# A fused attention and feed-forward kernel: the last product's lower half in two column halves, one tail store in one transfer, five stores in two

## The chip, the cores and the metric

The kernel runs on one core of a Trainium2 chip. A core has a matrix engine (TensorE, "PE" in the profile; its weight loads are listed apart as "PEld"), a vector engine (VectorE, "DVE"), a scalar engine (ScalarE, "ACT"), GpSimd ("POOL") and SyncE ("SP"), which does nothing here but issue transfers and wait. Transfers go through 16 DMA engines that the issuing queues share. The metric is the device time of one execution in microseconds (us). Before the change it is 294.83 us, the median of three runs (294.2 to 295.05).

## The reference

Eight batches of eight heads, 576 positions, head size 64. Attention looks back over a window of 64 positions; its output, 4608 rows of 512, goes through a feed-forward block with a squared ReLU.

```python
def attention(q, k, v):                 # (8, 8, 576, 64) each
    scores = np.matmul(q, k.transpose(0, 1, 3, 2)) / np.sqrt(64)
    rel = pos[:, None] - pos[None, :]
    scores = np.where((rel >= 0) & (rel < 64), scores, -1e9)
    attn = np.exp(scores - scores.max(-1, keepdims=True))
    return np.matmul(attn / attn.sum(-1, keepdims=True), v)

x = attention(q, k, v).transpose(0, 2, 1, 3).reshape(4608, 512)
h = np.maximum(x @ w_in, 0.0)           # w_in: 512 x 2048
out = (h * h) @ w_out                   # w_out: 2048 x 512
```

## The kernel before

The 4608 rows are worked in nine groups of 512. Groups 0 to 7 are the first 512 positions of each batch; group 8 holds the last 64 positions of all eight batches, two batches to a block of 128 rows. For each group the attention comes first (36 tiles of 128 rows in all), then the up-product into PSUM (`U`, line 482, in group 0, `UPm`, line 515, after it), ReLU on ScalarE and a square on ScalarE or VectorE, and then the down-product (`out_seven`, line 664).

The down-product treats 512 x 2048 times 2048 x 512 as two-by-two blocks and forms the result from seven block products instead of eight. The seven are listed in `plan` (line 738): a PSUM bank, the stationary operand, the moving one, and what is evicted after it. Sums of blocks of h are made on VectorE (`hsum`), sums of blocks of w_out once at the start. Each block product (`product`, line 685) is 16 matmuls: eight steps of K by two blocks `m` of 128 rows, 256 columns wide. `evac` (line 716) adds a bank to earlier sums and writes the result to one of three output buffers, `osb_all`; a buffer holds 256 rows of 512 columns, as two blocks of 128 rows.

`store` (line 703) sends a buffer to the output. In groups 0 to 7 it is one transfer of 512 KB from SP for each of the group's two halves (`row`), 16 transfers in all (line 706). In group 8, whose 128-row blocks hold 64 rows of each of two batches, every store is two transfers, 64 partitions each: one from SP, one from ScalarE's queue (line 712).

The last product of all is product 6 of group 8. Only there `by_rows` is set: all eight steps for the upper 128 rows come first, then all eight for the lower 128, and the two halves sit in different PSUM tiles (`split`). Each half is evicted on its own, 128 x 256, and stored on its own.

The order in which instructions are recorded is written out by hand in the string `ORDER` (line 15); each word is one step, and each engine works its own instructions in that order. `hs` is a sum, `Z` a half of a block product, `ev` an eviction, `sd` and `sh` a store. The last words are

```
Z8.5.1 sh8.1.1 Z8.6.0 ev8.5 Z8.6.1 sh8.0.1 ev8.6.0 sh8.1.0.0 ev8.6.1 sh8.1.0.1
```

So the last four are: evict and store the upper 128 rows of the last block, evict and store the lower 128. The waits are set by the layer that records the kernel: an instruction waits for a count of another engine's, and a transfer from SP or ScalarE's queue raises one of eight semaphores, taken in turn in the order of recording. A transfer also waits until the transfer eight before it, on the same semaphore, has landed. At the end SP waits for all eight in their order, drains, and all engines meet in a barrier (line 840).

Of the kernel before, what the change touches and what calls it, by code (L numbers as in the profile page):

```python
# [12 lines left out]
ALU = mybir.AluOpType  # L13
# [84 lines left out]
def kernel(  # L98
# [12 lines left out]
    nc = tc.nc  # L111
    B, H, S, D = q.shape
    NT, DM = out.shape
    DFF = moe_w_in.shape[1]
    P = 128
    HP = H // 2
    W_SCALE = 128.0
    OUT_SCALE = 1.0 / (W_SCALE * W_SCALE)
# [3 lines left out]
    NTB = NT // 512  # L122
# [3 lines left out]
    KH = FFC // 2  # L126
    NH = DM // 2
# [206 lines left out]
    def psum_of(kind):  # L334

        if kind in held:
            return held.pop(kind)
        if kind == "att":
            return ps_att.tile([P, 2, 512], FP32, name="att", tag="ps_a")
        if kind == "any":  # L340
            turns.append(len(turns) % 2)
            return psum_of(("up", "out")[turns[-1]])
        pool, tag = (ps_up, "ps_u") if kind == "up" else (ps_out, "ps_o")
        taken[kind] += 1
        return pool.tile([P, 512], FP32, name=tag, tag=tag)
# [295 lines left out]
    def next_osb():  # L641
        osbs.append(len(osbs) % 3)
        return osb_all[:, osbs[-1]]
# [20 lines left out]
    def out_seven(g):  # L664
        h2 = h2s[g]
        TH = 256
        top = (slice(0, TH), slice(0, KH)), (slice(0, TH), slice(KH, FFC))
        bot = (slice(TH, 512), slice(0, KH)), (slice(TH, 512), slice(KH, FFC))
        A = [[h2[:, ks, ts] for ts, ks in row] for row in (top, bot)]
        Sh = [hs_all[:, i] for i in range(2)]  # L670
        Sh += [A[1][0], A[0][1]]
        banks, sums, osb = {}, {}, {}

        def hsum(i, half, e=1):
            ks = slice(half * KH // 2, (half + 1) * KH // 2)
            x, y, op = ((A[1][0], A[1][1], ALU.add), (Sh[0], A[0][0], ALU.subtract),
                        (A[0][0], A[1][0], ALU.subtract), (A[0][1], Sh[1], ALU.subtract))[i]
            (nc.gpsimd, nc.vector)[e].tensor_tensor(  # L678
                out=Sh[i][:, ks], in0=x[:, ks], in1=y[:, ks], op=op)

        def split(bank):

            return g == NTB - 1 and bank == "D"

        def product(bank, a, w, half, first, by_rows):
            if first and half == 0:
                t = psum_of("up" if bank == "E" else "out")[:].rearrange("p (m d) -> p m d", m=2)
                banks[bank] = [t[:, m] for m in range(2)]
                if split(bank):
                    banks[bank][1] = psum_of("up")[:, 0:NH]  # L690
                else:
                    banks[bank].append(t)
            steps = [(kk, m) for kk in range(half * KH // 2, (half + 1) * KH // 2)
                     for m in range(2)]
            if by_rows:
                steps = [(kk, half) for kk in range(KH)]
            for kk, m in steps:
                nc.tensor.matmul(  # L698
                    banks[bank][m], a[:, kk, m * P:(m + 1) * P], w[:, kk],
                    start=(first and kk == 0 and (m == 0 or split(bank))), stop=(kk == KH - 1),  # L700
                    skip_group_check=True)

        def store(row, cols, ms):
            if g < NTB - 1:
                r0 = g * S + row * TH
                nc.sync.dma_start(
                    out=out[r0:r0 + TH, cols].rearrange("(m p) d -> p m d", p=P),
                    in_=osb[row][:, :, cols])
            else:
                tails = out.rearrange("(m j r) d -> j r m d", j=2, r=S)  # L710
                for j in range(2):
                    (nc.sync, nc.scalar)[j].dma_start(
                        out=tails[j, S - 64:S, 2 * row + ms.start:2 * row + ms.stop, cols],
                        in_=osb[row][64 * j:64 * j + 64, ms, cols])

        def evac(bank, to, add=None, row=0, col=0, ms=slice(0, 2)):
            if to == "osb":
                if row not in osb:
                    osb[row] = next_osb()
                dst = osb[row][:, ms, col * NH:(col + 1) * NH]  # L720
            else:
                sums[to] = stage.tile([P, 2, NH], FP32, name=to, tag="st")
                dst = sums[to][:]
            if ms == slice(0, 2):
                src, other = banks[bank][2], sums[add][:] if add else None
            else:
                src, other = banks[bank][ms.start], sums[add][:, ms.start]
                dst = dst[:, 0]
            if add is None:
                nc.scalar.activation(out=dst, in_=src, func=AF.Copy, scale=OUT_SCALE)  # L730
            else:
                nc.vector.scalar_tensor_tensor(  # L732
                    out=dst, in0=src, scalar=OUT_SCALE, in1=other, op0=ALU.mult, op1=ALU.add)

        W = [[w_out_sb[:, 0:KH, 0:NH], w_out_sb[:, 0:KH, NH:DM]],
             [w_out_sb[:, KH:FFC, 0:NH], w_out_sb[:, KH:FFC, NH:DM]]]
        last = g == NTB - 1
        plan = [
            ("A", A[0][0], W[0][0], True, (("A", "p1"),)),
            (("E", A[0][1], W[1][0], True, (("E", "osb", "p1", 0, 0),)) if last else  # L740
             ("A", A[0][1], W[1][0], False, (("A", "osb", None, 0, 0),))),
            ("B", Sh[1], wb[0], True, (("B", "u2", "p1"),)),
            ("C", Sh[0], W[0][1], True, (("C", "u4", "u2"),)),
            ("D", Sh[2], wb[1], True, (("D", "osb", "u4", 1, 1),)),
            ("C", Sh[3], W[1][1], False, (("C", "osb", "u2", 0, 1),)),
            ("D", A[1][1], wb[2], False, (("D", "osb", "u2", 1, 0),)),
        ]

        def mult(n, half):
            bank, a, w, first, _ = plan[n]  # L750

            product(bank, a, w, half, first, last and n == 6)

        def evacs(n, m=None):
            for e in plan[n][4]:
                if m is None and not split(e[0]):
                    evac(*e)
                for i in range(2) if m is None and split(e[0]) else () if m is None else (m,):
                    evac(*e, ms=slice(i, i + 1))

        def send(row, col=None, m=None):
            store(row, slice(0, DM) if col is None else slice(col * NH, (col + 1) * NH),
                  slice(0, 2) if m is None else slice(m, m + 1))

        return hsum, mult, evacs, send
# [3 lines left out]
    def seven(g):  # L769
        if g not in sevens:  # L770
            sevens[g] = out_seven(g)
        return sevens[g]
# [72 lines left out]
```

## Time and profile before

| | us |
|---|---|
| median of three runs | 294.83 |
| profiled execution, its own time | 295.02 |
| its span, first to last instruction | 293.3 |
| TensorE busy | 283.8 (97%) |
| VectorE busy | 202.4 (69%) |
| ScalarE busy | 190.7 (65%) |
| GpSimd busy | 107.2 (37%) |
| granted clock of TensorE | 1.0 |

The span runs from the first instruction to the last; the execution's own time has 1.7 us more around it. A row of a timeline is: start, duration (both us), engine ("q" behind it for a queue that issues), line of the kernel, operation, output and inputs, shape, count. A row of a DMA answer is: transfer, queue, count, size, and the us from its issue to its landing. A row of the stretches ("285.00:290.00 ...") has the busy time of each engine, then TensorE's granted clock, the mean busy share of the 16 DMA engines and the GB/s that they moved. A row of groups has the busy time of a group and, behind the comma, the mean ns of one.

### The profile page before, as it was taken

The numbers are of one execution on the slowest core, as the hardware profiler recorded it, in microseconds if no ns is written. First come the engines' busy times: TensorE is split into PE (matmuls) and PEld (weight loads), VectorE is DVE, ScalarE is ACT, GpSimd is POOL, SyncE is SP. The second block draws the span as 40 slices with busy tenths as digits, with TensorE's granted clock in tenths as the row PEclk, the third lists the DMA queues.
The fourth block names the chain that finished last, engine by engine and source line by source line (L and its number), as shares of the span: only waits on it lengthen the run. The fifth ranks groups of instructions, "written<-read, shape, count | busy, mean of one in ns | idle before, by whom it ended". The sixth has DMA issues, their size and how long they took to land.

```text
span 293.3 us, 7351 instructions
## 1 busy us (share of the span) xinstructions
PE 283.8 (97%) x2957; PEld 189.6 (65%) x2957; DVE 202.4 (69%) x362; ACT 190.7 (65%) x310; POOL 107.2 (37%) x164
## 2 busy tenths in 40 slices
PE   8879999999999999999999999999999999999994
PEld 3546676657876477556666676575765667865683
DVE  2696877989866789678836884886565746833572
ACT  3867888794345963687776928557856977156710
POOL 2559111674363436356446344463224400000000
PEclk9999999999999999999999999999999999999999
DMA  7999999887899999999997999799999931301114
GB/s 215 301 258 274 195 196 213 187 185 173 215 210 222 229 234 213 228 212 251 213 205 162 251 248 187 180 233 251 201 207 296 219 35 74 107 2 72 72 34 111
DMA packets 163617, 55.52 MB, mean 189 GB/s; under 512 B 149248, under 2 KB 159488, under 8 KB 163584
## 3 DMA queue, kind: packets, MB, share of 16 engines
q1 hardware_dynamic: 156400, 49.82, 77.2%
q0 software_dynamic: 5280, 4.19, 9.0%
q10 hardware_dynamic: 1904, 1.05, 1.2%
q8 instruction: 23, 0.38, 0.5%
q14 instruction: 10, 0.08, 0.1%
HBM read 38.80 MB, written 9.44 MB: 164 GB/s over the span
## 4 chain that ended last, share of the span: by engine, by line
PE 60%; DVE 0%; issue 0%
PE ps_u L518 29%; PE ps_o L698 26%; PE att L443 2%; PE att L418 2%; PE ps_u L698 1%; DVE osb_all L732 0%
## 5 line engine op out<-in xcount | busy, mean ns | idle before, releaser
L518 PE MATMUL ps_u<-xT,w_in_sb 128*128 128x512 f16 x512 | 122.2, 379 | 0.3
L497 ACT ACTIVATE hrelu<-ps_u 128x512 f32<-128x512 f32 x136 | 80.1, 593 | 53.3 <-PE ps_u L518 50.4
L698 PEld LDWEIGHTS <-h 128*128 128x128 f16 x720 | 69.5, 98 | 16.6
L518 PEld LDWEIGHTS <-w_in_sb 128*128 128x128 f16 x512 | 48.6, 98 | 48.0 <-issue 2.1
L512 DVE SCALAR_TENSOR_TENSOR h<-ps_u,hrelu 128x512 f16<-128x512 f32 x55 | 37.6, 687 | 29.1 <-ACT hrelu L497 28.8
L508 ACT ACTIVATE h<-hrelu 128x512 f16<-128x512 f32 x85 | 53.0, 629 | 2.2
L698 PE MATMUL ps_o<-w_out_sb,h 128*128 128x256 f16 x416 | 52.2, 273 | 0.0
L425 ACT ACTIVATE pm<-att 128x1024 f16<-128x1024 f32 x36 | 35.9, 1021 | 8.5 <-PE att L418 8.4
L264 POOL CAST v_ev<-v_st 128x512 f16<-128x512 f32 x34 | 22.7, 668 | 43.4 <-DMA v_st<-in_v_dram 27.2
L698 PE MATMUL ps_o<-wb_all,h 128*128 128x256 f16 x272 | 35.3, 273 | 0.0
L264 POOL CAST k<-k_st 128x512 f16<-128x512 f32 x32 | 22.6, 707 | 32.3 <-DMA k_st<-in_k_dram 28.5
L698 PEld LDWEIGHTS <-hs_all 128*128 128x128 f16 x288 | 28.1, 98 | 6.6 <-issue 0.3
L264 POOL CAST q<-q_st 128x512 f16<-128x512 f32 x28 | 19.8, 707 | 31.2 <-DMA q_st<-in_q_dram 30.1
L430 DVE TENSOR_TENSOR pm<-pm,mask_inner 128x1024 f16<-128x1024 f16 x28 | 23.1, 827 | 10.3 <-ACT pm L425 10.0
L264 POOL COPY v_od<-v_ev 64x512 f16<-64x512 f16 x40 | 28.5, 714 | 2.5
L450 DVE TENSOR_TENSOR x_sb<-att,rden 128x512 f16<-128x512 f32 x36 | 24.9, 691 | 1.2
L732 DVE SCALAR_TENSOR_TENSOR osb_all<-ps_o,u 128x512 f32<-128x512 f32 (+1 forms) x27 | 18.0, 667 | 10.3 <-PE ps_o L698 10.1
L678 DVE TENSOR_TENSOR hs_all<-h 128x1024 f16<-128x1024 f16 x18 | 13.4, 747 | 8.0 <-ACT h L508 8.0
L698 PE MATMUL ps_o<-wb_all,hs_all 128*128 128x256 f16 x144 | 18.3, 273 | 0.0
L698 PE MATMUL ps_o<-w_out_sb,hs_all 128*128 128x256 f16 x144 | 17.7, 272 | 0.1
L678 DVE TENSOR_TENSOR h<-h,hs_all 128x1024 f16<-128x1024 f16 x18 | 13.8, 779 | 2.7 <-PE ps_o L698 2.4
L443 PEld LDWEIGHTS <-pm 128*64 128x64 f16 x576 | 11.0, 110 | 7.0 <-issue 4.3
(86 smaller groups left out, 251.8 us busy)
## 6 DMA issues: line engine op xcount, KB each, us to landing
k_st<-in_k_dram SPq DMA_DIRECT2D x39, 256.0 KB, 4.2
v_st<-in_v_dram SPq DMA_DIRECT2D x39, 256.0 KB, 4.5
q_st<-in_q_dram SPq DMA_DIRECT2D x32, 256.0 KB, 4.3
out_dram<-osb_all SPq DMA_DIRECT2D x16, 512.0 KB, 3.9
w_out_sb<-in_moe_w_out_dram POOLq DMA_DIRECT2D x4, 512.0 KB, 14.0
w_in_sb<-in_moe_w_in_dram POOLq DMA_DIRECT2D x4, 256.0 KB, 6.1
w_in_sb<-in_moe_w_in_dram POOLq DMA_DIRECT2D x2, 512.0 KB, 9.1
q_st<-in_q_dram SPq DMA_DIRECT2D x8, 128.0 KB, 3.7
```

What stands on the lines that cost most here:

```text
L264: (nc.gpsimd, nc.vector)[e].tensor_copy(out=dst, in_=src)
L425: nc.scalar.activation(out=pms[i][:, part], in_=scs[i][:, part], func=AF.Exp, scale=1.0 / float(D) ** 0.5)
L430: nc.vector.tensor_tensor(out=pms[i][:, part], in0=pms[i][:, part], in1=mask[:].rearrange("p (o a) b r -> p o (a b r)", o=1) .to_broadcast ...
L443: nc.tensor.matmul(avs[i][64 * blk:64 * blk + 64, h // 4, h % 4, 0:65], pms[i][:, h % 2, h0:h0 + 64], vv[:, h, 0:65], start=True, stop=True)
L450: nc.vector.tensor_tensor(out=x_of(i)[:, :, i % 2, :].rearrange("p (a b) (c d) -> p a b c d", a=2, c=2), in0=avs[i][:, :, :, 0:D].rearrang ...
L497: nc.scalar.activation(out=hr_of[key][:], in_=src, func=AF.Relu)
L508: nc.scalar.activation(out=dst, in_=hr, func=AF.Square)
L512: nc.vector.scalar_tensor_tensor(out=dst, in0=hps, scalar=0.0, in1=hr, op0=ALU.max, op1=ALU.mult)
L518: nc.tensor.matmul(hps, w_in_sb[:, c, f * P:(f + 1) * P], xT_of(g)[:, :, c, :], start=(c == 0), stop=(c == DMC - 1))
L678: (nc.gpsimd, nc.vector)[e].tensor_tensor(out=Sh[i][:, ks], in0=x[:, ks], in1=y[:, ks], op=op)
L698: nc.tensor.matmul(banks[bank][m], a[:, kk, m * P:(m + 1) * P], w[:, kk], start=(first and kk == 0 and (m == 0 or split(bank))), stop=(kk ...
L732: nc.vector.scalar_tensor_tensor(out=dst, in0=src, scalar=OUT_SCALE, in1=other, op0=ALU.mult, op1=ALU.add)
```

## The change

There are three edits, all in the down-product and its stores.

1. In the last product, the lower 128 rows are computed in two column halves: eight matmuls of 128 columns for columns 0 to 127, then eight for columns 128 to 255. Their eviction is two instructions of 128 x 128.
2. The store of the upper 128 rows of the last block, the last but one, is one transfer from SP that takes all 128 partitions, in place of one from SP and one from ScalarE's queue.
3. The last five of the 512 KB stores (second half of group 5, both halves of groups 6 and 7) are two transfers of 256 KB each, both from SP.

```diff
+        def column_parts(ends):
+            return [slice(i, i + P) for i in range(0, NH, P)] if ends else [slice(0, NH)]
...
-            for kk, m in steps:
-                nc.tensor.matmul(
-                    banks[bank][m], a[:, kk, m * P:(m + 1) * P], w[:, kk],
-                    start=(first and kk == 0 and (m == 0 or split(bank))), stop=(kk == KH - 1),
-                    skip_group_check=True)
+            for c in column_parts(by_rows and half):
+                for kk, m in steps:
+                    nc.tensor.matmul(
+                        banks[bank][m][:, c], a[:, kk, m * P:(m + 1) * P], w[:, kk, c],
+                        start=(first and kk == 0 and (m == 0 or split(bank))),
+                        stop=(kk == KH - 1), skip_group_check=True)
 
         def store(row, cols, ms):
             if g < NTB - 1:
                 r0 = g * S + row * TH
-                nc.sync.dma_start(
-                    out=out[r0:r0 + TH, cols].rearrange("(m p) d -> p m d", p=P),
-                    in_=osb[row][:, :, cols])
+                parts = 2 if 2 * g + row >= 2 * NTB - 7 else 1
+                for m in range(0, 2, 2 // parts):
+                    nc.sync.dma_start(
+                        out=out[r0 + m * P:r0 + (m + 2 // parts) * P, cols]
+                        .rearrange("(m p) d -> p m d", p=P),
+                        in_=osb[row][:, m:m + 2 // parts, cols])
             else:
                 tails = out.rearrange("(m j r) d -> j r m d", j=2, r=S)
-                for j in range(2):
-                    (nc.sync, nc.scalar)[j].dma_start(
-                        out=tails[j, S - 64:S, 2 * row + ms.start:2 * row + ms.stop, cols],
-                        in_=osb[row][64 * j:64 * j + 64, ms, cols])
+                m = slice(2 * row + ms.start, 2 * row + ms.stop)
+                if (row, ms) == (1, slice(0, 1)):
+                    nc.sync.dma_start(out=tails[:, S - 64:S, m.start, cols],
+                                      in_=osb[row][:, 0, cols])
+                else:
+                    for j in range(2):
+                        (nc.sync, nc.scalar)[j].dma_start(
+                            out=tails[j, S - 64:S, m, cols],
+                            in_=osb[row][64 * j:64 * j + 64, ms, cols])
...
+            elif (row, col, ms) == (1, 0, slice(1, 2)):
+                for c in column_parts(True):
+                    nc.vector.scalar_tensor_tensor(
+                        out=dst[:, c], in0=src[:, c], scalar=OUT_SCALE, in1=other[:, c],
+                        op0=ALU.mult, op1=ALU.add)
```

## The prediction

> **What bounds the kernel now.** I read the page's busy table and its chain first, then the end of the chain in order of time, then the two queues that issue the last stores, then what follows the last landing.
>
> ```profile
> span 293.3 us, 7351 instructions
> PE 283.8 (97%) x2957; PEld 189.6 (65%) x2957; DVE 202.4 (69%) x362; ACT 190.7 (65%) x310; POOL 107.2 (37%) x164
> ...
> PE 60%; DVE 0%; issue 0%
> ```
>
> TensorE is busy for 97% of the span. From 200 us on, a list of its waits is empty: nothing holds it up there. So an edit that costs TensorE no column and does not starve it can only move what comes after its last column. That tail, from the chain of waits:
>
> ```profile
> 288.27 0.89 PE ps_u L698 x8
> 289.16 0.02 issue
> 289.18 0.42 DVE osb_all L732
> ```
>
> TensorE stops at 289.16, VectorE's last eviction ends at 289.60, and the span ends at 293.3. Of the 9.5 us without TensorE, 4.1 lie here. What happens in them, from the timelines of the SP and ACT queues (two rows each), the DMA answers of the same two moments, and the closing line's instructions:
>
> ```profile
> 288.84 0.56 SPq L712 DMA_DIRECT2D out_dram<-osb_all  x1
> 289.63 0.49 SPq L712 DMA_DIRECT2D out_dram<-osb_all  x1
> ```
> ```profile
> 288.88 0.80 ACTq L712 DMA_DIRECT2D out_dram<-osb_all  x1
> 289.78 0.56 ACTq L712 DMA_DIRECT2D out_dram<-osb_all  x1
> ```
> ```profile
> out_dram<-osb_all SPq DMA_DIRECT2D x1, 64.0 KB, 2.4
> out_dram<-osb_all ACTq DMA_DIRECT2D x1, 64.0 KB, 2.6
> ```
> ```profile
> out_dram<-osb_all SPq DMA_DIRECT2D x1, 64.0 KB, 2.3
> out_dram<-osb_all ACTq DMA_DIRECT2D x1, 64.0 KB, 2.3
> ```
> ```profile
> L840 SPq EVENT_SEMAPHORE  x6: 28/28/28, 292.1 to 292.4; - x6
> L840 SPq DRAIN  x1: 13/13/13, 292.5 to 292.5; - x1
> ```
>
> The first row of each queue is the store of the last block's upper 128 rows (last but one, four rows of 1 KB for each of 16 DMA engines in either half), the second that of its lower 128. ACT issues its last transfer 0.15 us after SP, because its issue before ran to 289.68. It lands at 289.78 + 2.3 = 292.1; SP then passes six closing waits in 0.4 us (0.06 each), drains at 292.5, and the barrier of all engines takes the other 0.8.
>
> **The change, part by part.**
>
> *Two column halves on TensorE.* Eight matmuls of 256 columns become sixteen of 128, each with its own weight load. The nearest rows of 128 columns with a load each are the transposes of line 461.
>
> ```profile
> 288.11 1.04 PE L698 MATMUL ps_u<-wb_all,h 128*128 128x256 f16 x8
> ```
> ```profile
> 83.81 0.61 PE L461 MATMUL att<-ident,x_sb 128*128 128x128 f16 x8
> ```
> ```profile
> L461 PEld LDWEIGHTS <-x_sb x48: 95/98/98, 12.8 to 84.1; 128*128 128x128 f16 x48
> L461 PE MATMUL att<-ident,x_sb x32: 219/219/229, 28.1 to 84.2; 128*128 128x128 f16 x32
> ```
>
> Eight take 0.61 us with 0.219 for the last, so one starts each 0.056 us. Sixteen then take 15 x 0.056 + 0.22 = 1.06 against 1.04: **+0.02 us**. Bounds: 0, and +0.65 if each had to wait out its own load of 0.098 (15 x 0.098 + 0.22 = 1.69). I take the transposes, the same shape. A page of the Trainium skill speaks against this: "TensorE: Matmul & The Clock Gate", section "Back-to-back issue gap", gives about 81 ns for a sustained stream of 128-column matmuls with loads. By it the sum would be 15 x 0.025 = 0.4 us later; the eight of this trace at 0.056 do not agree, but they are only eight.
>
> *Two halves on VectorE.* The first half was to be evicted while TensorE does the second. In the built program it does not: the first half's eviction waits for the count that the sixteenth matmul gives, and the second half waits for nothing more. So both follow TensorE's end, where one of 256 columns did.
>
> ```profile
> L732 DVE SCALAR_TENSOR_TENSOR osb_all<-ps_o,u 128x512 f32<-128x512 f32 x25 | 17.2, 686 | 9.4 <-PE ps_o L698 9.1
> L732 DVE SCALAR_TENSOR_TENSOR osb_all<-ps_u,u 128x256 f32<-128x256 f32 x2 | 0.8, 419 | 0.4 <-PE ps_u L698 0.4
> ```
> ```profile
> 285.58 0.42 DVE L732 SCALAR_TENSOR_TENSOR osb_all<-ps_o,u 128x256 f32<-128x256 f32 x1 [0.77 <-PE ps_o L698]
> 285.92 0.41 DVE L732 SCALAR_TENSOR_TENSOR osb_all<-ps_u,u 128x256 f32<-128x256 f32 x1
> ```
>
> The 256 columns between 419 and 686 ns cost 267, so 128 columns cost 419 - 134 = 285, and two 0.57. Two neighbours overlap by 0.08 (the second starts 0.34 after the first). 0.57 - 0.08 - 0.42 = +0.07; with a margin for the second not overlapping, **+0.10**. Ends: 0 (half the work each) and +0.42 (full price each).
>
> *The last store but one in one transfer, on SP.* ACT loses its issue at 288.88, so its last issue goes out with SP's: **-0.15**. SP's own issue, of 128 KB instead of 64, must end by 289.6:
>
> ```profile
> L712 SPq DMA_DIRECT2D out_dram<-osb_all x5: 489/596/665, 283.6 to 289.6; - x5
> ```
>
> The longest of its five (three of 128 KB) is 0.67, so 288.84 + 0.67 = 289.5 is in time, and nothing is queued behind it but the last store.
>
> But the transfer has another shape. Every plain transfer of before has 32, 64 or 128 as its first dimension on both sides; this one writes [2, 64, 256 columns], with the two batches first, from 128 partitions. No row of before shows how a first dimension of two is dealt over the DMA engines. Bounds: as all others, eight rows for each of 16 engines; or one share for each of its two first entries, that is 64 rows on each of two engines. The rate of one engine, from stretches in which the stores had all 16:
>
> ```profile
> 288.45:288.60 0.15, 0.15 (x4) 0.14 (x2) 0.15 (x1) 0.00 (x0) 0.00 (x0) 1.00 1.12 396
> 290.00:291.40 1.40, 0.00 (x0) 0.00 (x0) 0.00 (x0) 0.00 (x0) 0.00 (x0) 1.00 0.95 291
> 284.95:285.65 0.70, 0.70 (x9) 0.63 (x7) 0.07 (x1) 0.00 (x0) 0.00 (x0) 1.00 0.87 177
> ```
>
> The last two columns are the 16 engines' share and GB/s: 396, 291 and 177 GB/s are 24.8, 18.2 and 11.1 for one engine, or 41, 56 and 93 ns for a row of 1 KB. Spread over 16, the store costs four more rows each, 0.2 us, under the last store's flight: 0. On two engines it lands 60 rows later than the 2.4 us of SP's half: 2.5, 3.4 or 5.6 us. With 14 engines idle I stay near the fast row, 45 ns: 2.7. It then lands at 288.84 + 2.4 + 2.7 = 293.9, and the four rows that the last SP store has on each of those engines come behind it, +0.2: 294.1, where the last landing is 292.1 now. I take the two engines: I know of no transfer in this trace that would have to be cut inside an entry of its first dimension to make 16 equal shares, and this one would. The Trainium skill's "DMA: Bandwidth & Descriptors", section "Why a DMA increments its semaphore by 16 and not by 1", states it as a rule: the engine count is the largest up to 16 that divides the slowest dimension of both sides, here 2. No run here shows it yet.
>
> *Five mid-size stores in two transfers each.* The first stands in a full SP queue, the four others on an idle one:
>
> ```profile
> 220.97 1.32 SPq L706 DMA_DIRECT2D out_dram<-osb_all  x1
> 222.33 1.97 SPq L178 DMA_DIRECT2D k_st<-in_k_dram  x2
> ...
> 228.53 1.21 SPq L178 DMA_DIRECT2D v_st<-in_v_dram  x2
> ...
> 231.99 1.25 SPq L400 DMA_TRANSPOSE qT<-q  x1
> ...
> 244.25 0.39 SPq L706 DMA_DIRECT2D out_dram<-osb_all  x1
> 252.55 1.23 SPq L468 DMA_TRANSPOSE xT<-x_sb  x1
> 253.88 21.01 SPq L706 DMA_DIRECT2D out_dram<-osb_all  x3
> ```
> ```profile
> 245.83 0.64 PE L418 MATMUL att<-qT,kT 64*128 64x64 f16 x32
> ```
>
> ```profile
> qT<-q SPq DMA_TRANSPOSE x14, 4.0
> ```
>
> Each of the four others issues 0.4 us more before a gap of 8 us or more, in which SP waits for VectorE. The one at 220.97 sets all behind it back by 0.6 (a 256 KB issue, half of the row at 228.53) to 1.3 us. The first to need what comes last is the score product at 245.83, whose transposed q is issued at 231.99 and lands about 4.0 us later (236): 9 us of cover. Cost 0; without the cover, up to 1.3. The store's buffer is written again two stores later, some 20 us on.
>
> There is one more effect, of the count: stores and loads take eight semaphores in turn, SP's closing waits go through them in the order 0 to 7, and five more transfers and one fewer move the last two from 2 and 3 to 6 and 7. Four waits of 0.06 then lie before the last landing and not behind it: **-0.24**.
>
> **Sum.** Apart from the store's shape: +0.02 + 0.10 - 0.15 - 0.24 = -0.27 us. With two engines: the last landing 294.1 on semaphore 7, then one wait and the drain (0.08) and the barrier (0.83), so the span ends at 295.0, against 293.3: **+1.7 us**, and the evictions' terms are covered by it. The profiled execution took 295.02, the median is 294.83; I put the difference on the median: 296.5.
>
> **Rivals.**
>
> *Not slower: the store is spread over 16 engines.* Then it lands by 291.5 and the other terms stand: 294.83 - 0.27 = 294.56. For it: all transfers of before come out evenly. Against: none of them has this shape. It decides as soon as at least about eight engines share the work (16 rows each, 12 more than now, 0.5 us, still before the last store).
>
> *TensorE slower at 128 columns, the store spread.* With a start each 0.098 us, the end comes 0.63 later: -0.27 + 0.63 = +0.36, 295.2. Against it the row at 83.81. With two engines it changes nothing, as the store lands last.
>
> *One engine, or the slow rate.* At 93 ns the two engines need 5.6 instead of 2.7: +4.6 us, 299.4; one engine with all 128 rows comes to about the same. Against: those 93 ns were seen with all engines at work.
>
> *The fifth mid-size store starves TensorE.* It decides from a delay of 9 us on; the issue rows give 1.3. If it did, each us past 9 is one us.
>
> **Chances.** Two engines near the fast rate 0.60; spread over 16, 0.29; spread with slow matmuls 0.05; the slow rate or one engine 0.04; starving 0.02. Within 0.3% (0.88 us, about what a measurement of this kernel can tell from no change) lie both spread cases and a sliver of the first (0.04, if its rows start before the store ahead is done); at 41 ns it is +1.5, 0.5%. So slower 0.61, same 0.36, faster 0.03. The first case's own range is 296.1 to 297.4 (41 to 56 ns, and a few tenths for the runs' spread); the range that also takes in the spread case goes down to 294.4, and up to 297.5.
>
> **What will show it.** Right: the 128 KB issue of the new store line lands about 5 us after it, the DMA share of the last 2 us is near 2/16, and the closing waits end on that landing. Both eviction halves start after the last matmul; ACT's last issue starts within 0.05 of SP's. Wrong: a landing within 2.7 us, with the span near 293.0; or waits of TensorE between 225 and 280 us.

## The result, and the profile after

The changed kernel takes 297.43 us, the median of six runs (297.21 to 297.71); the kernel before took 294.69 (294.2 to 295.25) in six runs beside it. The ratio is 1.0092, with a 95% interval of 1.0078 to 1.0105: slower by 0.9%, or 2.7 us. The profiled execution took 297.71, its span is 296.0, against 293.3 before.

From the page, and the end of the chain of waits:

```profile
span 296.0 us, 7374 instructions
PE 283.5 (96%) x2965; PEld 189.7 (64%) x2965; DVE 202.7 (68%) x363; ACT 190.5 (64%) x310; POOL 109.2 (37%) x164
```
```profile
288.15 0.91 PE ps_u L703 x16
289.06 0.02 issue
289.08 0.29 DVE osb_all L746
289.38 0.20 DVEq L858
```

TensorE does the same work in the same time and ends at 289.06, where it ended at 289.16 before. The 2.7 us all lie behind its last column: 4.1 us from there to the end of the span before, 7.0 now. What happens in them, in the timeline of SP's queue (its last two issues) and of ACT's (its last), and in the DMA answers for the windows of the last store but one and of the last stores:

```profile
288.73 0.62 SPq L721 DMA_DIRECT2D out_dram<-osb_all  x1
289.60 0.53 SPq L725 DMA_DIRECT2D out_dram<-osb_all  x1
```
```profile
289.61 0.52 ACTq L725 DMA_DIRECT2D out_dram<-osb_all  x1
```
```profile
out_dram<-osb_all SPq DMA_DIRECT2D x1, 128.0 KB
```
```profile
out_dram<-osb_all SPq DMA_DIRECT2D x1, 64.0 KB, 5.5
out_dram<-osb_all ACTq DMA_DIRECT2D x1, 64.0 KB, 5.1
```

The issues are where they were forecast: ACT's last starts 0.01 us after SP's. The landings are not. The last SP store lands 5.5 us after its issue, at 289.60 + 5.5 = 295.1; the same store took 2.3 before. For the single store the profile gives no landing; it has to be read from SP's closing waits (line 858 here, line 840 before). First the waits of SP near the end, after and before, then the closing line's instructions after:

```profile
SPq L858 <- DMA out_dram<-osb_all: 4.4, 2, 3.9
```
```profile
SPq L840 <- DMA out_dram<-osb_all: 1.8, 2, 1.3
```
```profile
L858 SPq EVENT_SEMAPHORE  x3: 28/28/28, 294.9 to 295.1; - x3
L858 SPq DRAIN  x2: 7/10/13, 295.2 to 295.2; - x2
```

SP stood 4.4 us in two waits for the stores, 1.8 before. The first of the last three waits, the one for the single store, passes at 294.9, 6.2 us after the issue at 288.73; the second is for ACT's last store, which had landed by then; the third, for the last SP store, passes at 295.1. How many DMA engines did it? Three stretches of after, then three of before (the last two columns are the 16 engines' busy share and GB/s):

```profile
289.60:290.40 0.80, 0.00 (x0) 0.00 (x0) 0.00 (x0) 0.00 (x0) 0.00 (x0) 1.00 0.94 245
290.65:291.50 0.85, 0.00 (x0) 0.00 (x0) 0.00 (x0) 0.00 (x0) 0.00 (x0) 1.00 0.09 20
...
292.80:293.50 0.70, 0.00 (x0) 0.00 (x0) 0.00 (x0) 0.00 (x0) 0.00 (x0) 0.60 0.14 50
293.80:294.60 0.80, 0.00 (x0) 0.00 (x0) 0.00 (x0) 0.00 (x0) 0.00 (x0) 0.50 0.07 24
```
```profile
289.60:290.40 0.80, 0.00 (x0) 0.00 (x0) 0.00 (x1) 0.00 (x0) 0.00 (x0) 1.00 0.96 238
290.40:291.60 1.20, 0.00 (x0) 0.00 (x0) 0.00 (x0) 0.00 (x0) 0.00 (x0) 1.00 0.79 247
291.60:292.10 0.50, 0.00 (x0) 0.00 (x0) 0.00 (x0) 0.00 (x0) 0.00 (x0) 1.00 0.00 0
```

Before, all is moved by 291.6 at a share of 0.79 and more. After, the share is 0.14 from 292.8 (two engines of 16 are 0.125, and a row's record is 46 ns long where rows start 42 ns apart), then 0.07 (one is 0.0625). There is a second count. Each engine that works on a transfer writes one packet of 4 bytes for it, so the packets under 512 bytes count engines. From 289.55 on, after and before:

```profile
DMA packets 527, 0.47 MB, mean 73 GB/s; under 512 B 66, under 2 KB 527, under 8 KB 527
```
```profile
DMA packets 582, 0.50 MB, mean 112 GB/s; under 512 B 96, under 2 KB 582, under 8 KB 582
```

96 are six transfers of 16; 66 are four of 16 and one of 2. The single store ran on two engines.

### The profile page after: what moved, and what is told of

Its sections match the earlier page's. It is cut to its first block, busy times and chain, and to the rows that moved or that the text cites. A ratio compares the mean times of both kernels' runs of the same rounds, so it can differ in the third digit from the quotient of the medians.

```text
span 296.0 us, 7374 instructions
## 1 busy us (share of the span) xinstructions
PE 283.5 (96%) x2965; PEld 189.7 (64%) x2965; DVE 202.7 (68%) x363; ACT 190.5 (64%) x310; POOL 109.2 (37%) x164
## 4 chain that ended last, share of the span: by engine, by line
PE 59%; DVE 0%; DVEq 0%; issue 0%
PE ps_u L518 29%; PE ps_o L703 26%; PE att L443 2%; PE att L418 2%; PE ps_u L703 1%; DVE osb_all L746 0%; DVEq L858 0%
## 5 line engine op out<-in xcount | busy, mean ns | idle before, releaser
L264 POOL CAST v_ev<-v_st 128x512 f16<-128x512 f32 x34 | 23.4, 688 | 42.9 <-DMA v_st<-in_v_dram 30.8
L264 POOL CAST k<-k_st 128x512 f16<-128x512 f32 x32 | 23.2, 728 | 31.3 <-DMA k_st<-in_k_dram 30.3
L264 POOL CAST q<-q_st 128x512 f16<-128x512 f32 x28 | 19.0, 680 | 31.5 <-DMA q_st<-in_q_dram 31.4
L264 POOL COPY v_od<-v_ev 64x512 f16<-64x512 f16 x40 | 29.6, 741 | 2.5
L430 DVE TENSOR_TENSOR pm<-pm,mask_inner 128x1024 f16<-128x1024 f16 x28 | 23.9, 857 | 9.6 <-ACT pm L425 9.5
L678 DVE TENSOR_TENSOR h<-h,hs_all 128x1024 f16<-128x1024 f16 x18 | 13.1, 736 | 2.9 <-PE ps_o L703 2.6
```

The lines of the kernel that those rows point to most:

```text
L264: (nc.gpsimd, nc.vector)[e].tensor_copy(out=dst, in_=src)
L430: nc.vector.tensor_tensor(out=pms[i][:, part], in0=pms[i][:, part], in1=mask[:].rearrange("p (o a) b r -> p o (a b r)", o=1) .to_broadcast ...
L678: (nc.gpsimd, nc.vector)[e].tensor_tensor(out=Sh[i][:, ks], in0=x[:, ks], in1=y[:, ks], op=op)
```

## The experiments

Times are medians; each ratio is to runs of the kernel before on the same chip, with its 95% interval. Where one tail is compared with another, it is measured from the end of TensorE's last matmul to the end of the span, because the time up to that end differs between executions by more than the effects looked for (288.07 us in the trace of e4, 289.14 in that of before; the rows of the chain above put it up to 0.02 later). In this measure before has 4.15 us and after 6.96; each of these tails is from one trace.

### e1: all of the change but the single store

```diff
-                if (row, ms) == (1, slice(0, 1)):
+                if False:
                     nc.sync.dma_start(out=tails[:, S - 64:S, m.start, cols],
...
```

> The changed kernel with the last store but one again in two transfers of 64 partitions (SP and ACT); column halves and the five split stores stay. Theory (the [2, 64, 256] transfer runs on two DMA engines and is all of the loss): this store lands within 2.7 us, the last landing is ACT's at about 292.1, on semaphore 7, and the span ends near 293.0; 294.4 us, 3.0 below the changed kernel and 0.3 below before. Rival (the column halves or the split stores carry the loss): it stays above 296.

Measured: 294.4 us against 294.59, ratio 0.9988 (0.9972 to 1.0004). The tail is 3.93. The last two stores in the DMA answer:

```profile
out_dram<-osb_all SPq DMA_DIRECT2D x1, 64.0 KB, 2.0
out_dram<-osb_all ACTq DMA_DIRECT2D x1, 64.0 KB, 2.2
```

With the store cut in two again the landings are back at 2.0 and 2.2, and the loss is gone. (One point was not as expected: SP's last store is on the first of the eight semaphores here, so that all eight closing waits follow its landing.) Column halves and five split stores together cost nothing that can be measured.

### e2: the single store alone

```diff
+                if (row, ms) == (1, slice(0, 1)):
+                    nc.sync.dma_start(out=tails[:, S - 64:S, m.start, cols],
+                                      in_=osb[row][:, 0, cols])
+                else:
...
```

> The kernel before with the one-transfer store alone. Theory: the store lands about 6.2 us after its issue at 288.8, that is at 295.0, the last SP store behind it at 295.2; its semaphores are 0 to 2, so up to six closing waits follow: span 296.4, 297.8 us. Rival (the store is hidden, the loss lies in the other edits): 294.5 to 294.9.

Measured: 297.92 us against 294.59, ratio 1.0097 (1.0077 to 1.0118). The DMA answers for the single store and for the last stores, and SP's closing wait:

```profile
out_dram<-osb_all SPq DMA_DIRECT2D x1, 128.0 KB
```
```profile
out_dram<-osb_all SPq DMA_DIRECT2D x1, 64.0 KB, 5.6
out_dram<-osb_all ACTq DMA_DIRECT2D x1, 64.0 KB, 5.3
```
```profile
SPq L858 <- DMA out_dram<-osb_all: 4.9, 1, 4.9
```

The whole loss comes from this one edit. Its tail is 7.36, 0.4 longer than after's: without the split stores the last transfers are on early semaphores, so that six closing waits are left at the last landing where after has one. From that landing to the end of the span e2 has 1.21 us and after 0.91, which is 0.3 of the 0.4.

### e3: the first dimension as a dial

The stores of groups 6 and 7 stand on an idle SP queue. Each is cut into its two blocks of 128 rows, and each half is written with another first dimension: 16 and 8, 64 and 4, 128 and 2, 2 and 128.

```diff
+                lead = {(6, 0): (16, 8), (6, 1): (64, 4), (7, 0): (1, 2), (7, 1): (2, 1)}
+                if (g, row) in lead:
+                    for m, n in enumerate(lead[g, row]):
+                        nc.sync.dma_start(
+                            out=out[r0 + m * P:r0 + m * P + P, cols]
+                            .rearrange("(r a) d -> a r d", a=n),
+                            in_=osb[row][:, m, cols])
...
```

(The entry 1 leaves the plain form, with the 128 rows first. The SBUF side has its 128 partitions first in all eight.)

> The kernel before with the four stores of groups 6 and 7 in two halves of 128 rows of 2 KB, the output side of the halves written with a first dimension of 16 and 8, 64 and 4, 128 and 2, 2 and 128 (rows of a half land in another order, so those rows of the output are permuted; nothing else is changed). Theory (as many engines as the largest number up to 16 that divides the first dimension): from issue to landing 2.3 us for 16, 64 and 128, and with about 0.085 us for each further row per engine 3.0 for 8, 4.3 for 4 and 7 for 2. Rival (the shape does not matter, the queue or the place at the tail does): all eight land within 2.2 to 2.7 us.

Measured: 294.38 us in one run, about as before, which is no surprise, as all four pairs lie under other work. What counts here are the transfers themselves. Four DMA answers, for the pairs 16 and 8, 64 and 4, 128 and 2, and 2 and 128, and a stretch in the middle of the third pair:

```profile
DMA packets 281, 0.54 MB, mean 59 GB/s; under 512 B 24, under 2 KB 24, under 8 KB 280
...
out_dram<-osb_all SPq DMA_DIRECT2D x2, 256.0 KB, 2.9
```
```profile
DMA packets 277, 0.54 MB, mean 65 GB/s; under 512 B 20, under 2 KB 20, under 8 KB 276
```
```profile
DMA packets 274, 0.52 MB, mean 49 GB/s; under 512 B 18, under 2 KB 18, under 8 KB 274
...
out_dram<-osb_all SPq DMA_DIRECT2D x2, 256.0 KB, 2.1
```
```profile
DMA packets 275, 0.54 MB, mean 59 GB/s; under 512 B 18, under 2 KB 18, under 8 KB 274
...
out_dram<-osb_all SPq DMA_DIRECT2D x2, 256.0 KB, 7.7
```
```profile
267.00:271.00 4.00, 4.00 (x27) 2.44 (x26) 1.31 (x2) 3.36 (x6) 0.00 (x0) 1.00 0.13 47
```

24 is 16 + 8, 20 is 16 + 4, and 18 is 16 + 2, in either order. (The profile gives a landing only for transfers on all 16 engines, so an answer has that of one of its two.) With a first dimension of two, 128 rows of 2 KB go at 47 GB/s with a share of 0.13, two engines; the same bytes with 128 first land in 2.1 us. In the last pair the plain half is issued behind the two-engine half and lands after 7.7 us instead of 2.1: it has rows on those two engines as well, and they come last. So the first dimension sets the engines, as the Trainium skill states ("DMA: Bandwidth & Descriptors", section "Why a DMA increments its semaphore by 16 and not by 1"); these counts agree with it, though only powers of two were tried. The times agree less well. The halves on 16 engines landed after 2.9 (16), 2.5 (64) and 2.1 us (128), where 2.3 was expected. By the packet records the last 4-byte packet of a half on fewer engines came 3.8 (8), 5.7 (4) and 7.4 us (2) after its issue, where landings at 3.0, 4.3 and 7 were expected.

### e4: the same 128 KB from SP alone, in two transfers

```diff
-                    nc.sync.dma_start(out=tails[:, S - 64:S, m.start, cols],
-                                      in_=osb[row][:, 0, cols])
+                    for j in range(2):
+                        nc.sync.dma_start(out=tails[j, S - 64:S, m, cols],
+                                          in_=osb[row][64 * j:64 * j + 64, ms, cols])
```

> The changed kernel with the last store but one in two transfers of 64 partitions that both go out from SP. Theory (two engines): each lands about 2.4 us after its issue; SP's last store is issued at 290.0 instead of 289.6 and lands at 292.3 on semaphore 0, with seven closing waits behind it: span 293.6, 295.0 us. Rival (128 KB from one queue is what is slow): the landings are past 294, as in the changed kernel, and the time is above 297.

Measured: 294.95 us against 294.59, ratio 1.0003 (0.9986 to 1.0021). The DMA answer for the two, and SP's issue of the last store:

```profile
out_dram<-osb_all SPq DMA_DIRECT2D x2, 64.0 KB, 2.2
```
```profile
289.04 0.55 SPq L726 DMA_DIRECT2D out_dram<-osb_all  x1
```

The rival that it is the one queue, and not the shape, falls: the same bytes from the same queue land in 2.2 us. What one queue costs is the order of issue. TensorE ended at 288.07 in this run, so SP's last issue comes 0.97 us behind it instead of 0.55, and the tail is 4.32.

### e5: the column halves alone

```diff
+            for c in column_parts(by_rows and half):
...
+                        banks[bank][m][:, c], a[:, kk, m * P:(m + 1) * P], w[:, kk, c],
...
+            elif (row, col, ms) == (1, 0, slice(1, 2)):
+                for c in column_parts(True):
...
```

> The kernel before with the column halves alone. Theory: both evictions follow the sixteenth matmul, the second ends about 0.49 us after the first starts where one of 256 columns took 0.42, and TensorE takes 0.02 more; but ACT's last issue was late anyway (its queue is free 0.09 us after VectorE's end), so the last landing does not move: 294.6 us, 0 to 0.1 above before. Rival (the first half is evicted under the second half's matmuls): VectorE ends 0.13 earlier and the second eviction alone follows TensorE. Second rival (a 128-column matmul starts each 0.081 us): TensorE's last piece is 0.4 us longer.

Measured: 294.69 us against 294.7, ratio 0.9995 (0.9985 to 1.0005); tail 4.16. The reason shows in the timelines of after (matmuls and evictions of the last 128 rows):

```profile
287.99 1.06 PE L703 MATMUL ps_u<-wb_all,h 128*128 128x128 f16 x16
```
```profile
289.08 0.49 DVE L746 SCALAR_TENSOR_TENSOR osb_all<-ps_u,u 128x128 f32<-128x128 f32 x2 [0.47 <-PE ps_u L703]
```

Both evictions come after the sixteenth matmul, and the two take 0.49 where one took 0.42. The 0.07 lies under ACT's issue of the store before. ACT's last two issues in e5:

```profile
288.55 1.45 ACTq L725 DMA_DIRECT2D out_dram<-osb_all  x2
```

They run back to back, so that the last goes out when it did before, 0.62 us after TensorE's end (0.64 before).

### e6: four stores split

```diff
+                parts = 2 if 2 * g + row >= 2 * NTB - 6 else 1
+                for m in range(0, 2, 2 // parts):
...
```

> The kernel before with four of the 512 KB stores in two transfers each (groups 6 and 7; the one in the full queue stays whole) and nothing else. Theory: the last two transfers take the semaphores 6 and 7 instead of 2 and 3, so two steps of 0.06 us instead of six follow ACT's landing, -0.24: 294.35 us. Rival (the split stores change nothing): from ACT's landing to the end of the span 1.21 us as before.

Measured: 294.34 us against 294.7, ratio 0.9989 (0.9975 to 1.0004). Only the four stores on the idle queue are split; the last two transfers then sit on later semaphores. The closing line:

```profile
L858 SPq EVENT_SEMAPHORE  x4: 27/28/28, 291.0 to 291.6; - x4
```

Two waits, at 291.58 and 291.64, are left at the last landing, where before had six in 0.4 us. From the first of them to the end of the span are 0.97 us, 1.20 before: -0.23, where -0.24 was expected. The tail is 3.94 against 4.15. The time agrees in sign, but its interval holds 1.

### e7 and e10: a PSUM tile for each column half, with e6

```diff
-                    banks[bank][1] = psum_of("up")[:, 0:NH]
+                    banks[bank][1] = [psum_of("up")[:, 0:P], psum_of("att")[:, 0, P:NH]]
...
```

The matmuls write, and the evictions read, the half's own tile, so that the first half can leave while TensorE does the second.

> As the four split stores alone, and the lower 128 rows of the last bank lie in two PSUM tiles, one for each column half, from the product that opens the bank on (eight more matmuls of 128 columns there), so that the first half's eviction waits for its own eight matmuls. Theory: the first half is evicted under the second's matmuls, VectorE ends 0.31 us after TensorE instead of 0.44; but ACT's last issue stays where its queue sets it, so the last landing and the time do not move against the four split stores: 294.35 us. Rival (VectorE's end sets the last landing): 0.1 less, 294.2.

> The kernel of the two PSUM tiles and four split stores once more, in five rounds, since its interval was too wide to tell it from before: from TensorE's end to the span's end it had 3.70 us against 4.15, so 0.45 less, 0.9985 of before.

Measured: e7 294.39 us against 294.7, ratio 0.9991 (0.9973 to 1.0008); e10 294.55 against 294.72, ratio 1.0000 (0.9983 to 1.0018). The timelines of e10, TensorE then VectorE then ACT:

```profile
288.97 0.61 PE L706 MATMUL att<-wb_all,h 128*128 128x128 f16 x8
```
```profile
289.17 0.29 DVE L756 SCALAR_TENSOR_TENSOR osb_all<-ps_u,u 128x128 f32<-128x128 f32 x1
289.62 0.29 DVE L756 SCALAR_TENSOR_TENSOR osb_all<-att,u 128x128 f32<-128x128 f32 x1 [0.15 <-PE att L706]
```
```profile
289.30 1.46 ACTq L735 DMA_DIRECT2D out_dram<-osb_all  x2
```

Now the overlap is there: the first half is evicted under the second half's matmuls, and VectorE ends 0.33 us after TensorE instead of 0.46. But ACT's two issues of 1.46 us in a row start at 289.30, so its last starts at 290.21, 0.63 after TensorE's end, as before. The tails, 3.70 and 3.74, are the shortest of all, 0.2 shorter than e6's, and that was not expected. ACT's last store landed 2.1 us after its issue, in e6 after 2.3; why was not tried. The times cannot be told from before.

### e8: own tiles, five split stores, and the last store but one from SP and GpSimd

```diff
...
+                if (row, ms) == (1, slice(0, 1)):
+                    for j in range(2):
+                        (nc.sync, nc.gpsimd)[j].dma_start(
+                            out=tails[j, S - 64:S, m, cols],
+                            in_=osb[row][64 * j:64 * j + 64, ms, cols])
```

> The changed kernel with column halves in two PSUM tiles, five split stores, and the last store but one in two transfers of 64 partitions, from SP and from GpSimd's queue instead of ACT's. Theory: ACT's queue is free, so both last issues follow VectorE's end at once, 0.1 earlier than before for SP and 0.25 for ACT, and the closing waits end on semaphores 6 and 7: -0.5, 294.1 us, if GpSimd's transfer lands before 291.8. Rival (GpSimd's transfer is slow to issue and lands last): the span ends about 1 us after that landing.

Measured: 294.79 us against 294.7, ratio 0.9993 (0.9978 to 1.0008). GpSimd's issue, and the landings of its store and of the last two:

```profile
289.86 0.56 POOL L732 DMA_DIRECT2D out_dram<-osb_all  x1 [55.21 <-DVE osb_all L758]
```
```profile
out_dram<-osb_all POOLq DMA_DIRECT2D x1, 64.0 KB, 2.6
out_dram<-osb_all SPq DMA_DIRECT2D x1, 64.0 KB, 2.7
out_dram<-osb_all ACTq DMA_DIRECT2D x1, 64.0 KB, 2.8
```

ACT is freed: its last issue starts 0.36 after TensorE's end instead of 0.63. It gains nothing: 294.1 us was expected, on the condition that GpSimd's transfer lands before 291.8, and it landed at 292.5. GpSimd issues 0.50 later than SP (289.86 against 289.36), and the last stores land in 2.8 and 2.7 instead of 2.3 us; the tail is 4.18. That GpSimd's transfer, still in flight while the last stores move, slows these down is likely, but was not shown.

### e9: the five split stores alone

```diff
+                parts = 2 if 2 * g + row >= 2 * NTB - 7 else 1
+                for m in range(0, 2, 2 // parts):
...
```

> The kernel before with the five split stores alone. Theory: nothing of them reaches TensorE; the last two transfers take the semaphores 7 (ACT) and 0 (SP), so SP's landing at about 2.75 us after TensorE's end starts all eight closing waits, and the drain comes 0.08 earlier than before: 294.6 us, TensorE's end to the span's end 4.07 instead of 4.15. Rival (the split store in the full queue makes TensorE wait): a wait of TensorE between 225 and 260 us.

Measured: 294.51 us against 294.72, ratio 0.9996 (0.9983 to 1.0009); tail 3.96. The fifth, in the full queue, and the transposes behind it in SP's timeline:

```profile
221.73 1.91 SPq L713 DMA_DIRECT2D out_dram<-osb_all  x2
...
233.84 1.26 SPq L400 DMA_TRANSPOSE qT<-q  x1
```

The pair issues for 1.91 us where one took 1.32, and the transposed q goes out at 233.84, 12.1 us after the store's issue (11.0 before). It has still 12 us to the score product at about 246, and the list of TensorE's waits between 225 and 260 is empty (in after, from 200 to its end).

## Why the prediction was right, and where it was off

It forecast 296.5 us, slower, by one mechanism; measured were 297.43 and that mechanism. The size was forecast less well: 2.7 us slower, where 1.7 was expected. 297.43 lies just above the first case's own range (296.1 to 297.4) and 0.07 below the upper end of the whole range (297.5), so that it was luck that the range held. Its width came from the rate of a row, and that rate was near its fast end; what took up the room was a term that the sum did not have. Step by step:

*Two engines.* Right, in all its parts: two small packets instead of 32, a share near 2/16, then the closing waits ending on that landing. e2 shows that this edit alone makes the loss, e1 that the rest makes none, e3 that it is the first dimension, e4 that it is not the queue. The rival in which the store is spread over 16 engines is out, and so is that of slow matmuls (sixteen took 1.06 us).

*Its size.* This is the term that was off. Predicted was a landing 2.4 + 2.7 = 5.1 us after the issue; measured are 6.2. The rate was right: 50 GB/s on two engines (the stretch from 292.80) are 25 for one, a row of 1 KB each 0.041 us, where 0.045 was taken. The rest can be read from the packet records, which carry no engine but can be told apart by their spacing. One of the two engines starts at 290.47 and goes at 0.042 a row almost at once. The other begins with four rows at 290.63, 290.90, 291.20 and 291.50, of 0.22 to 0.25 us each, and comes to 0.042 only at 291.75; that costs it 1.12 - 4 x 0.042 = 0.95 us. It also takes ACT's last four rows in turn with its own, 0.17. So: 288.73 + 1.90 to its first row + 64 x 0.042 + 0.95 + 0.17 = 294.44, and 0.46 more until the wait passes at 294.9. Against the forecast of 5.1 us the rate gave 0.2 less, the first rows with their landing 0.1 more, and the slow start (0.95) and ACT's rows (0.17) the rest; these two stood nowhere in the sum. The prediction had a slow rate as a separate rival, over the whole transfer, and none in which one engine starts slowly. The last stretch above is this engine working alone.

*The closing waits.* One is left at the last landing, where six were. From that landing to the end of the span are 0.91 us, 1.20 before: -0.29. The sum had just this (0.08 and 0.83); its -0.24 belongs to the other case, with ACT's landing last, and e6 gave -0.23. The tail adds up: the last landing comes 3.09 us later, measured from TensorE's end (6.05 against 2.96), and less 0.29 that is 2.80, the difference of the tails. Forecast was +2.0 for the landing.

*Columns on TensorE.* +0.02, as taken: 1.06 us for sixteen against 1.04 for eight. The 81 ns of the Trainium skill's "TensorE: Matmul & The Clock Gate" ("Back-to-back issue gap") would make it, as an estimate, 15 x 0.081 + 0.22 = 1.43; the trace does not agree with it here, with one start each 0.056 over sixteen.

*Two eviction halves.* +0.07 (0.49 against 0.42), where 0.10 was taken; both after the last matmul, as read from the built program. It was meant to overlap, and e7 and e10 show that it can with a tile for each half.

*ACT freed.* Its last issue starts 0.01 after SP's instead of 0.15, but SP's is itself 0.07 later for the evictions, so that the gain is 0.08 (0.64 to 0.56 after TensorE's end), where 0.15 was taken. In after it is hidden by the late landing.

*Five split stores.* 0, as taken (e9). SP's full stretch moved by 1.1 us behind the fifth store, within the 0.6 to 1.3 read from the issue rows, and no wait of TensorE followed.

So the 0.29 us that the change gained at the closing waits stand against 3.1 us by the shape of one transfer, and ACT's 0.08 did not reach the end.

## What to carry to other kernels

Before two transfers are joined into one, look at the first dimension that the joined one has: 128 KB written as [2, 64, 256] ran on two of 16 DMA engines and landed 6.2 us after its issue, the two halves of 64 rows in 2.2 to 2.6. In the last microseconds of a kernel, where nothing hides a landing, count the 4-byte packets per transfer in the profile: they are the engines that it got. (The profile counts all packets under 512 bytes, so this needs a window without data in rows as short as that.) And an earlier end of one step (an eviction in halves, a queue with one issue fewer) is worth only what the other queue's last issue leaves of it, which was nothing measurable here.

## What the runs showed that was not expected

One of the two engines moved its first four rows at about 0.3 us a row and then went on at 0.042. It is so in e2 too (rows at 290.65, 290.94, 291.24 and 291.54, of 0.23 to 0.25 us), so it is no accident of one run; in e3's third pair both engines took 0.2 to 0.4 us for single rows in the first 2 us, where later rows of 2 KB took 0.08. The cause was not looked for and stays open.

The last stores' rows on the other 14 engines came late as well, though these engines were idle: from 290.65 to 291.50 the share was 0.09, where before moved 247 GB/s from 290.40 to 291.60, and their rows were done only by about 292.7, against 291.6. This did not set the end, and its cause stays open.

Two things in the profile look like news and are not: TensorE's granted clock falls to 0.5 after 293, when it has had nothing to do for 4 us; and the profile leaves the landing of a transfer on fewer than 16 engines blank (here those on 8, 4 and 2), which is no sign that it was early.
